# Transposes of q and k straight from the layout of their loads, a new order of the opening, and the second weights asked for ahead of a gate

## The chip, the cores and the metric

The kernel runs on one core of a Trainium2 chip. The metric is the device time of one execution in microseconds (us), the median of several runs; lower is better.

## The reference

Attention with a squared ReLU in place of a softmax, over 8 batches, 12 heads, 448 positions and 64 values a head; its output, laid out as 3584 rows of 768, goes through two weight matrices with a GELU between them. Inputs and output are float32.

```python
scores = scale * np.matmul(q, k.transpose(0, 1, 3, 2))      # scale = 1/sqrt(64)
attn = np.maximum(scores, 0.0) ** 2 / S                     # S = 448
x = np.matmul(attn, v)                                      # (8, 12, 448, 64)
x = x.transpose(0, 2, 1, 3).reshape(B * S, H * D)           # (3584, 768)
h = x @ w_in                                                # (3584, 2048)
out = (0.5 * h * (1.0 + erf(h / sqrt(2)))) @ w_out          # (3584, 768)
```

## The kernel before

**Work and tiles.** All products are in bfloat16. The loads from DRAM are issued by GpSimd (POOL), which converts float32 to bfloat16 on the way. A batch's 12 heads are three groups (g) of four. For each group there are 7 QK steps (L686), each one tile of 896 columns in PSUM; ACT (L698) or DVE (L700) takes the ReLU with the scale, DVE squares it (L707), and after 7 such steps TensorE does AV (L746). Two copies (L400, L402) put its result into `xT`, the transposed input of the first weight product. That product (L800, "F1": 16 atoms of 128 columns of `w_in` a batch, a GELU on ACT behind each) writes a ring `h_sb`. The product with `w_out` (L1203 at first, L1108 from then on) is done on 256 rows at a time, as seven products on sums of blocks in place of eight; the sums of the weights for it (`t_sb`, L1046) are made on DVE once `w_out` is there. For the last three batches the first product is done in that way too (L942, its weight sums at L867).

**Transposes.** QK needs q and k with the head dimension on partitions (`qT`, `kT`, two buffers each). Batches 0 and 1 are transposed on TensorE (L580, L608). From batch 2 on the DMA transposes, issued by SP, do it: three for k, one a group (L632), and four for q, one for each c of 4 (L641), with 128 values to a block. For these a block must hold two heads side by side in an order that the loads of L349 and L434 don't give. So for batch 2 DVE permutes q and k after their load (L529, L540: nine copies) into `pq` and `pk`; for batches 3 to 7 `add_wide` (L459) loads straight into the permuted order, with 6 loads for k and 12 for q a batch, and one for v.

**Order.** A scheduler writes out the order of all instructions when the program is built. The first 263 operations stand by hand in `ORDER` (L69): a letter for the engine (P TensorE, A ACT, D DVE, G POOL, S SP) and the number of the operation. It covers attention of batches 0 and 1, and the first product of batch 0. Every engine works through its own instructions in that order, and an instruction that waits holds up all behind it on its engine. After `ORDER` a planner with costs for each operation (those in `sch.add`), biases and due times picks the order on ACT, DVE and SP. TensorE's order from there on is a fixed list, `pe_q`: eight atoms of the first product of batch 1 (`LEAD`), then for each batch the slots of `slots` (QK, QK, AV, QK, QK; QK, QK, QK), with atoms of the two weight products shared out between them. POOL's list, `pool_q`, is fixed as well: it is the order in which loads are added. Up to eight loads of POOL are under way; the next waits for the landing of the eighth before it.

**Loads.** In POOL's list stand the loads of batch 0, parts of `w_in` between the loads of batch 1, those of batch 2 by group (k, q, v of g 0, 1, 2), the first part of `w_out` (4 of 16 row blocks), then `gate` (L653), a copy of four values of `qT`, with which POOL waits until batch 2 has been transposed, then the two other parts of `w_out` (6 row blocks each), then the loads of batch 3. From then on it goes on by batch: gate of batch b + 1, loads of batch b + 2.

The end of POOL's part of the list for batches 1 and 2 (L1316 to L1335):

```python
for g in range(G):
    add_load(2, g, g + 1)
add_wout(0)
add_steps(steps(1), ATT1_BIAS, True)
...
add_T_dma(2, [[]] * 7)
add_gate(2)
add_wout(1)
add_wout(2)
```

Of the kernel before, what the change touches and what calls it, by code (L numbers as in the profile page):

```python
# [23 lines left out]
FF = 2048  # L24
KD = DM // 128
# [10 lines left out]
T_TWO = 0.72  # L36
# [8 lines left out]
DMA_FREE = 4.54  # L45
# [11 lines left out]
NEAR = 0.5  # L57
# [4 lines left out]
WIDE = 2.0  # L62
# [13 lines left out]
G0 G1 G2 G3 G4 G5 A10 D13 G6 A16 P11 P14 G7 D12 A15 P17 G8 D18 P21 P39 D22 P33 P36 A34 D40  # L76
P19 D20 A37 P23 G9 P42 P48 D24 P54 A43 D35 A49 P51 D44 P25 D38 A52 D41 G117 A55 D53 P45 D50
A26 D47 A46 P57 D56 P69 P66 A58 D70 P27 G118 A67 P29 D59 P63 G119 A28 D71 P60 A64 G120 D68
P78 D61 A62 P75 A79 D65 P81 P31 D30 A76 D80 P96 G121 D32 A97 P72 D77 G122 A82 D98 P129 G123
D74 A73 P90 D130 P84 P108 A91 G124 D83 P131 A85 D109 P93 P141 D132 A94 D92 P102 D95 P105  # L80
P111 A103 D86 P143 D110 G125 A106 D104 P99 A112 D107 G126 A144 P87 D100 A101 D113 A142 P157
P114 D88 G127 A158 D89 P133 D115 A116 G128 P135 D159 A134 P160 P163 D136 P166 A164 P145 D167
A161 D165 P253 A146 D168 D162 P169 P172 G147 A254 P175 A173 D170 P245 G148 A176 D171 P255
A246 D177 G149 D174 P184 P187 A256 P196 A185 G150 D188 P137 P139 A138 P178 D197 G151 A140
D186 P193 P211 G152 D180 P247 A212 G153 D213 P249 A248 D179 A194 D198 G154 P263 A250 D195
D229 G155 P223 P220 A264 D189 P190 S235 A224 D221 P265 G156 A191 D225 P267 A266 D192 D222
P199 P217 A268 P214 D231 A218 P257 S236 D215 A200 D219 P259 A258 D216 D201 P181 P208 A260
P205 D230 A209 P261 D182 P251 D183 A262 D210 A206 D233 P202 A252 S237 D207 D232 P226 D234
A203 D204 S238 S239 P269
# [17 lines left out]
class Scheduler:  # L107
# [151 lines left out]

    def place(self, fixed):  # L260
# [14 lines left out]
        while rest or any(fixed.values()):  # L275
# [7 lines left out]
            for e, v in fixed.items():  # L283
                if v and not (e == "PE" and by.get("PE")):
                    tops.append(self.pick(v[:1]))
# [11 lines left out]
def kernel(  # L297
# [34 lines left out]
    q32 = natpool.tile([KC, 4, HC * D], F32, tag="pq", name="q32")  # L332
    k32 = natpool.tile([128, 2, NK * D], F32, tag="pk", name="k32")

    def get_nat(b):
        if b not in nq:

            tq, tk = ("pq", "pk") if b == 1 else ("nq", "nk")
            nq[b] = natpool.tile([KC, H, NC * D], BF16, tag=tq, name="nq")
            nk[b] = natpool.tile([128, HP, NK * D], BF16, tag=tk, name="nk")  # L340
            vt[b] = vpool.tile([128, HP, NK * D], BF16, tag="v", name="v_sb")

# [4 lines left out]
    def load_q(b, g0, g1, c0=0, c1=NC):  # L347
        get_nat(b)
        nc.gpsimd.dma_start(  # L349
            nq[b][:, 4 * g0 : 4 * g1, c0 * D : c1 * D], q_view(b, g0, g1, c0, c1)  # L350
        )
# [25 lines left out]
    pqk = []  # L377

    def get_p():
        if not pqk:  # L380
            pqk.append(natpool.tile([KC, NC, DM], BF16, tag="pq", name="pq"))
            pqk.append(natpool.tile([128, G, NK * 128], BF16, tag="pk", name="pk"))
        return pqk

# [3 lines left out]
    def get_T(b):  # L388
        if b not in qkT:
            qkT[b] = (  # L390
                tpool.tile([128, HP, S], BF16, tag="qT", name="qT"),
                tpool.tile([128, G, NK * 128], BF16, tag="kT", name="kT"),
            )
        return qkT[b]

# [24 lines left out]
    Pq, Pk, Tq, Tk = {}, {}, {}, {}  # L420
# [3 lines left out]
    def war(b):  # L424

        old = [o for (bb, *_), o in list(Pq.items()) + list(Pk.items()) if bb == b - 1]
        c = {1: -1, 2: 0}.get(b, b - 1)
        old += [o[0] for (bb, *_), o in list(Tq.items()) + list(Tk.items()) if bb == c]
        return old
# [19 lines left out]
    def add_v(b, g0, g1):  # L449
        def fn():  # L450
            get_nat(b)
            nc.gpsimd.dma_start(vt[b][:, 2 * g0 : 2 * g1], kv_view(v, b, g0, g1))  # L452

        old = [o for (bb, *_), o in AV.items() if bb == b - 3]
        o = dma(fn, (g1 - g0) * 4 * S * 256, old)
        for g in range(g0, g1):
            ld_v[b, g] = [o]

    def add_wide(b):  # L459


        def k_fn(e):
            def fn():
                to = get_p()[1].rearrange("p g (i e d) -> e p g i d", e=2, d=D)
                src = kv_view(k, b, 0, G).rearrange("p (g e) (i d) -> e p g i d", e=2, d=D)
                for g in range(G):
                    nc.gpsimd.dma_start(to[e][:, g], src[e][:, g])  # L467

            return fn

        def q_fn(e, j):
            def fn():
                to = get_p()[0].rearrange("p c (g j e d) -> j e g p c d", j=2, e=2, d=D)
                src = q[b].rearrange("(g e j) (p c) d -> j e g p c d", e=2, j=2, c=NC)
                for g in range(G):
                    nc.gpsimd.dma_start(to[j][e][g], src[j][e][g])  # L476

            return fn

        def v_fn():  # L480
            vt[b] = vpool.tile([128, HP, NK * D], BF16, tag="v", name="v_sb")
            nc.gpsimd.dma_start(vt[b], kv_view(v, b, 0, G))

        n = G * 4 * S * 256
        ks = [dma(k_fn(e), WIDE * n / 2, war(b), G) for e in range(2)]
        qs = [dma(q_fn(e, j), WIDE * n / 4, war(b), G) for e in range(2) for j in range(2)]
        old = [o for (bb, *_), o in AV.items() if bb == b - 3]
        o = dma(v_fn, n, old)
        ops = Both(ks), Both(qs)
        for g in range(G):  # L490
            ld_v[b, g] = [o]
            Pk[b, g] = ops[0]
            for c in range(NC):
                Pq[b, g, c] = ops[1]

    class Both:


        def __init__(self, ops):
            self.ops = ops  # L500

        @property
        def done(self):
            ends = [o.done for o in self.ops]
            return None if None in ends else max(ends)

    def add_load(b, g0=0, g1=G):
        if b > 2:
            return add_wide(b)
# [16 lines left out]

    def permute_k(copy, g, src):

        copy(  # L529
            get_p()[1][:, g].rearrange("p (i e d) -> p e i d", e=2, d=D),  # L530
            src.rearrange("p e (i d) -> p e i d", d=D),
        )

    def permute_q(copy, g, c0, c1, src):

        dst = get_p()[0][:, c0:c1, 256 * g : 256 * g + 256].rearrange(
            "p c (j e d) -> e p j c d", j=2, d=D
        )
        for e in range(2):
            copy(dst[e], src[:, 2 * e : 2 * e + 2].rearrange("p j (c d) -> p j c d", d=D))  # L540

    def add_pk(b, g0, g1, after=(), bias=0.0):
        for g in range(g0, g1):
            deps = ld_k[b, g] + list(after)
            deps += [Tk[max(b - 1, 1), x, i][0] for x in range(G) for i in range(NK)]
            Pk[b, g] = sch.add(
                (("DVE", 0.31, 0.43),),
                lambda e, g=g: permute_k(V.tensor_copy, g, nk[b][:, 2 * g : 2 * g + 2]), deps,
                bias=bias,
            )  # L550

    def add_pq(b, g0, g1, c0=0, c1=NC, after=(), bias=0.0):
        for g in range(g0, g1):
            deps = [ld_q[b, g, c] for c in range(c0, c1)] + list(after)
            deps += [Tq[max(b - 1, 1), g, c][0] for c in range(c0, c1)]
            if b == 2:
                deps += [Tq[1, x, c][0] for x in range(G) for c in range(NC)]
            d = 2 * (0.07 + (c1 - c0) * 128 / 3840)

            def fn(e, g=g):  # L560
                permute_q(
                    V.tensor_copy, g, c0, c1, nq[b][:, 4 * g : 4 * g + 4, c0 * D : c1 * D]
                )

            op = sch.add((("DVE", d, d + 0.12),), fn, deps, bias=bias)
            for c in range(c0, c1):
                Pq[b, g, c] = op
# [31 lines left out]
    def add_tq(b, g, c0=0, c1=NC, bias=T_BIAS):  # L599
# [14 lines left out]
        def fn2(e):  # L614
            copy(e, get_T(b)[0][:, 2 * g : 2 * g + 2, c0 * KC : c1 * KC], box[0])
# [11 lines left out]
    def add_T_dma(b, after):  # L627

        after = [list(x) for x in after]
        for g in range(G):  # L630
            def fn(e, g=g):
                nc.sync.dma_start_transpose(  # L632
                    get_T(b)[1][:, g].rearrange("p (i t) -> p i t", t=128), get_p()[1][:, g]
                )

            op = sch.add((("SP", 1.2, 3.0),), fn, [Pk[b, g]] + old_T(b) + after.pop(0), mode="X")
            for i in range(NK):
                Tk[b, g, i] = (op, op)
        for c in range(NC):
            def fn(e, c=c):  # L640
# [813 lines left out]
```

## Time and profile before

| | |
|---|---|
| median of 3 runs | 370.96 us (370.91 to 371.25) |
| the profiled execution | 370.77 us |
| its span, first to last instruction | 368.9 us |
| mean granted TensorE clock | 0.999 |
| busy: TensorE (PE), its weight loads (PEld) | 358.9, 222.1 us |
| busy: DVE, ACT, POOL | 288.3, 200.8, 108.0 us |
| POOL waiting at the gates, in total (5 times) | 64.4 us, the longest 19.2 |
| software DMA queue (POOL's loads) | 74992 packets, 22.47 MB, 58.6% |
| hardware DMA queue (transposes, stores) | 38768 packets, 19.46 MB, 26.8% |

The profile is of one execution. Busy times are those of the engine's own instructions; issuing a DMA takes an engine's queue but isn't counted for SP and ACT. The share of a DMA queue is the time that its packets took, in parts of 16 DMA engines over the stretch. A line such as `PE L686` is an instruction of line 686 on TensorE; `<-` names what the instruction waited for.

### The profile page before, as it was taken

The page shows a single profiled execution, that of the slowest core. Times are in us where ns is not written, and L with a number is a line of the kernel's source. Part 1 is how long each engine was busy: PE and PEld are TensorE (multiplying, and loading weights), DVE is VectorE, ACT ScalarE, POOL GpSimd, SP SyncE. Part 2 cuts the span into 40 slices and gives each one's busy share as a digit, 9 for nine tenths or more (in the row PEclk, how much of TensorE's full clock was granted, in tenths as well). Part 3 has the DMA queues.
Part 4 walks back from the last instruction along what each step waited for, and adds up shares of the span by engine and source line. Part 5 has one row for each costly group of instructions (what it writes and reads, how often), then busy time and mean ns, then how long its engine had stood idle before and what let it go on. Part 6 is the DMA issues. An engine that isn't in the chain of part 4 may idle for free.

```text
span 368.9 us, 8544 instructions
## 1 busy us (share of the span) xinstructions
PE 358.9 (97%) x3557; PEld 222.1 (60%) x3557; DVE 288.3 (78%) x493; ACT 200.8 (54%) x308; POOL 108.0 (29%) x149
## 2 busy tenths in 40 slices
PE   8799999999999999999999999999999999999994
PEld 7566645455544455544455545457886897688663
DVE  2998991789868978987699888888998658665862
ACT  4988865664447845677755588853440353044200
POOL 8666401726087096097095000000000000000000
PEclk9999999999999999999999999999999999999999
DMA  9999999999999999999999960003002301310233
GB/s 174 196 200 204 202 189 134 173 171 131 244 135 167 160 85 172 209 163 154 146 93 133 205 117 2 3 0 87 2 0 88 85 2 29 109 36 2 85 85 88
DMA packets 114166, 42.98 MB, mean 116 GB/s; under 512 B 92816, under 2 KB 110672, under 8 KB 114128
## 3 DMA queue, kind: packets, MB, share of 16 engines
q0 software_dynamic: 74992, 22.47, 58.6%
q1 hardware_dynamic: 38768, 19.46, 26.8%
q8 instruction: 28, 0.46, 0.5%
q10 hardware_dynamic: 368, 0.51, 0.4%
q14 instruction: 10, 0.08, 0.1%
HBM read 45.61 MB, written 11.01 MB: 153 GB/s over the span
## 4 chain that ended last, share of the span: by engine, by line
PE 87%; DMA 4%; DVE 4%; ACT 2%; POOL 1%; issue 1%; DVEq 0%; POOLq 0%; ACTq 0%
PE pso L1108 32%; PE psh L800 24%; PE pb L942 13%; PE ps L686 8%; PE pav L746 6%; PE pso L1203 3%; DMA v_sb<-in_v_dram 2%; DVE a_sq L707 2%; DMA nk<-in_k_dram 2%; ACT a_sq L698 2%; POOL nk L434 0%; POOL v_sb L452 0%; POOL nq L349 0%; PE tp L580 0%; DVE a_sq L700 0%
## 5 line engine op out<-in xcount | busy, mean ns | idle before, releaser
L698 ACT ACTIVATE a_sq<-ps 128x896 bf16<-128x896 f32 (+1 forms) x136 | 117.4, 914 | 44.6 <-PE ps L686 44.5
L707 DVE TENSOR_TENSOR a_sq<-a_sq 128x896 bf16<-128x896 bf16 (+1 forms) x169 | 97.5, 617 | 7.5 <-ACT a_sq L698 7.2
L800 PE MATMUL psh<-xT,win_sb 128*128 128x448 bf16 (+1 forms) x516 | 96.6, 340 | 0.1
L800 PEld LDWEIGHTS <-win_sb 128*128 128x128 bf16 x516 | 47.8, 98 | 45.5 <-issue 10.2
L810 ACT ACTIVATE h_sb<-psh 128x448 bf16<-128x448 f32 x80 | 43.9, 549 | 24.1 <-PE psh L800 23.9
L1108 PEld LDWEIGHTS <-s_sb 128*128 128x128 bf16 x424 | 40.6, 98 | 27.0 <-issue 2.2
L700 DVE TENSOR_SCALAR a_sq<-ps 128x896 bf16<-128x896 f32 x33 | 35.9, 1090 | 18.3 <-PE ps L686 17.8
L686 PE MATMUL ps<-qT,kT 64*64 64x448 bf16 (+1 forms) x756 | 47.3, 336 | 2.2 <-ACT qT L402 0.6
L976 DVE TENSOR_TENSOR part<-pb,part 128x448 f32<-128x448 f32 x60 | 34.6, 619 | 18.4 <-PE pb L942 18.4
L476 POOL DMA_DIRECT2D pq<-in_q_dram x60 | 41.8, 704 | 10.1 <-DVE a_sq L707 6.4
L1108 PEld LDWEIGHTS <-h_sb 128*128 128x128 bf16 x312 | 29.9, 98 | 21.1 <-issue 2.5
L1108 PE MATMUL pso<-wout_sb,s_sb 128*128 128x384 bf16 (+2 forms) x216 | 38.1, 320 | 0.3 <-DVE osb L1142 0.3
L1108 PE MATMUL pso<-wout_sb,h_sb 128*128 128x384 bf16 x208 | 38.1, 326 | 0.0
L1108 PE MATMUL pso<-t_sb,s_sb 128*128 128x384 bf16 x208 | 38.1, 326 | 0.0
L746 PE MATMUL pav<-a_sq,v_sb 64*64 64x448 bf16 (+1 forms) x756 | 36.8, 330 | 0.7 <-ACT a_sq L698 0.4
L686 PEld LDWEIGHTS <-kT 64*64 64x64 bf16 x756 | 18.3, 105 | 24.2 <-issue 17.4
L985 ACT ACTIVATE h_sb<-part 128x448 bf16<-128x448 f32 x36 | 19.8, 578 | 19.9 <-DVE part L976 19.8
L467 POOL DMA_DIRECT2D pk<-in_k_dram x30 | 28.9, 966 | 1.5 <-issue 0.9
L746 PEld LDWEIGHTS <-v_sb 64*64 64x64 bf16 x756 | 21.1, 107 | 13.0 <-issue 2.3
L942 PEld LDWEIGHTS <-win_sb 128*128 128x128 bf16 x288 | 27.6, 98 | 2.2 <-issue 0.4
L1142 DVE TENSOR_TENSOR osb<-pso,p_sb 128x384 f32<-128x384 f32 x39 | 21.7, 556 | 8.2 <-PE pso L1108 5.7
L400 DVE CAST xT<-pav 128x448 bf16<-128x448 f32 (+1 forms) x43 | 23.7, 583 | 4.6 <-PE pav L746 3.9
(62 smaller groups left out, 292.0 us busy)
## 6 DMA issues: line engine op xcount, KB each, us to landing
pk<-in_k_dram POOLq DMA_DIRECT2D x30, 112.0 KB, 4.4
pq<-in_q_dram POOLq DMA_DIRECT2D x60, 56.0 KB, 5.0
v_sb<-in_v_dram POOLq DMA_DIRECT2D x5, 672.0 KB, 9.1
out_dram<-osb SPq DMA_DIRECT2D x8, 336.0 KB, 3.0
wout_sb<-in_moe_w_out_dram POOLq DMA_DIRECT2D x2, 1152.0 KB, 12.1
v_sb<-in_v_dram POOLq DMA_DIRECT2D x9, 224.0 KB, 8.8
out_dram<-osb SPq DMA_DIRECT2D x7, 288.0 KB, 3.4
out_dram<-osb SPq DMA_DIRECT2D x8, 240.0 KB, 3.1
```

The source lines that it names most:

```text
L467: nc.gpsimd.dma_start(to[e][:, g], src[e][:, g])
L476: nc.gpsimd.dma_start(to[j][e][g], src[j][e][g])
L686: nc.tensor.matmul(ps[64 * j : 64 * j + 64, e, x * w : x * w + w], kT[r, g, i * 128 + 64 * j : i * 128 + 64 * j + 64], qT[r, 2 * g + j, co ...
L698: A.activation(ar, ps, AF.Relu, scale=c_att)
L700: V.tensor_scalar(ar, ps, c_att, 0.0, op0=mybir.AluOpType.mult, op1=mybir.AluOpType.max,)
L707: V.tensor_mul(box["a2"][:, :, :used], ar, ar)
L746: nc.tensor.matmul(pav[0][o2 : o2 + 64, e, :w], vt[b][r, 2 * g + e, bass.ts(i, D)], box["a2"][r, e, o : o + w], start=(i == 0), stop=(i == ...
L800: nc.tensor.matmul(ph[:, x * n : x * n + n], win_sb[:, kd, bass.ts(m + x, 128)], xT[b][:, kd, c], start=(kd == 0), stop=(kd == KD - 1),)
L810: A.activation(h_ring()[:, m : m + nm, o + c.start : o + c.stop], box[0][:, :S].rearrange("p (x n) -> p x n", x=nm), AF.Gelu,)
L942: nc.tensor.matmul(bank[name][:, y, z * HS : z * HS + HS], w[:, k, bass.ts(mm, 128)], right()[:, k], start=first and k == 0 and z == 0, st ...
L976: V.tensor_add(get(to), ps(name), get(other))
L1108: nc.tensor.matmul(box[bank][:, n0:n1], left()[:, kf], right[:, kf, n0:n1], start=bool(need) and kf == 0, stop=kf == K2 - 1, skip_group_ch ...
```

## The change

**Layout.** From batch 3 on q and k are loaded as batch 2's were, with one load each (`add_wide`, `Both`, `pq`, `pk`, the permutes and their DVE operations are gone). q gets a tile with one empty column block of 64 ahead of it and one behind; two memsets on POOL clear them. k is transposed with the heads as they lie: a block of 128 holds two neighbouring key blocks of one head (or the last of one head and the first of the next). q is transposed twice, once from the start of the tile and once 64 values further on, so that each q block lands once on the lower and once on the upper 64 partitions; the two results go to the even and odd slots of a `qT` of 49 slots. QK and AV pick their blocks by new indices; their number and sizes are the same.

**Transposes.** A batch has nine on SP in place of seven: for each group k, q from offset 64 ("even", 8 blocks) and q from offset 0 ("odd", 9, 8 and 8 blocks). A group's QK needs the three of its group (`even`, `odd`, and the odd one before). The planner's costs for one are 1.6 and 4.5 us in place of 1.2 and 3.0.

```diff
     def add_T_dma(b, after):
...
+        def turn(dst, src, deps):
+            return sch.add(
+                (("SP", T_STEP, T_TIME),),
+                lambda e: nc.sync.dma_start_transpose(dst(), src()),
+                deps + old_T(b) + after.pop(0), mode="X",
+            )
...
+        def q_src(n, o, k):
+            return lambda: nq[b][:, 128 * n + D * o : 128 * (n + k) + D * o]
...
+        n0, odd = 0, None
         for g in range(G):
...
+            op = turn(k_dst(g), k_src(g), list(ld_k[b, g]))
             for i in range(NK):
                 Tk[b, g, i] = (op, op)
...
+            n = 8 * g + 9
+            even = turn(slots_of(8 * g, 1, 8), q_src(8 * g, 1, 8), lands)
+            prior = odd or even
...
+            odd = turn(slots_of(n0, 0, n - n0), q_src(n0, 0, n - n0), lands + beyond)
+            n0 = n
+            for c, o in enumerate((even, odd, prior, odd)):
+                Tq[b, g, c] = (o, o)
```

**Gate and weights.** The gate copies one value of each of the 49 slots, so it waits for all nine transposes; for batch 2 it now stands behind the second and third part of `w_out`. The slots at which SP may start the transposes of a batch are the same two, five transposes at the first and four at the second (before: four and three).

```diff
     add_wout(0)
     add_steps(steps(1), ATT1_BIAS, True)
-    for g in range(G):
-        add_pk(2, g, g + 1, bias=T_TWO)
-        add_pq(2, g, g + 1, bias=T_TWO)
-    add_T_dma(2, [[]] * 7)
-    add_gate(2)
+    add_T_dma(2, [[]] * 9)
     add_wout(1)
     add_wout(2)
+    add_gate(2)
...
-            add_T_dma(b + 1, [at(b, n + (y >= 4)) for y in range(7)])
+            add_T_dma(b + 1, [at(b, n + (y >= 5)) for y in range(9)])
```

**Order.** `ORDER` is new, 257 operations long. It holds the same work of TensorE and the same loads in the same order of POOL; POOL's list behind it is the one above. Its SP words put five transposes of batch 2 in this order: S233 (q even, g 1), S232 (k, g 1), S230 (q even, g 0), S229 (k, g 0), S231 (q odd, g 0). Its beginning and its last lines:

```diff
+D13 G0 G1 A10 P11 G2 A16 D12 P17 P14 A18 P39 P42 P19 D15 A40 G3 D43 P21 G4 A22 D20 D41 P36 G5
+D44 G6 P54 P33 A37 P25 G7 P48 A34 P23 D55 A49 D24 D26 P51 P57 A52 P63 A58 G8 D56 D35 P69 G9
...
+P220 P214 A180 D207 P217 A244 P245 D183 A221 A215 P253 G153 G154 P211 D210 S230 A218 A246 P223 D186
+D222 A224 G155 D219 P202 A212 D216 A254 A204 D225 P259 P261 A260 P263 A262 A203 D213 S229 P255
+A264 P247 S231 A256 P257 P226 A248 A258 P265 G156
```

**Planner.** Its start of the DMA is 3.05 us in place of 4.54, and `NEAR` is 0.25 in place of 0.5. A new `pick_pe` may take the next atom of a weight product ahead of its turn when the next QK or AV in `pe_q` would wait.

```diff
+    def pick_pe(self, v):
...
+        top = self.pick(v[:1])
+        wait = math.inf if top is None else top[1] - self.free["PE"]
+        if v[0].mode == "F" or wait <= (PULL if self.mode == "F" else PULL_IN):
+            return top
+        nxt = next((o for o in v if o.mode == "F"), None)
+        other = nxt and self.pick([nxt])
+        if other and other[1] - self.free["PE"] <= PULL and other[1] < self.free["PE"] + wait:
+            return other
+        return top
```

**Buffers.** The float32 tiles of the start and the tiles of batch 1 lie in buffers of the weight sums (`t1`, `t2`, `t4`) and of `s1`; the weight sums of the first product take the q tile, the k tile and a `qT` buffer, so that they wait for the last QK of batch 6; v of batch 7 waits for AV of batch 5, and the block sums of batch 6 for the QK of batch 7.

```diff
-        old = [o for (bb, *_), o in AV.items() if bb == b - 3]
+        old = [o for (bb, *_), o in AV.items() if bb == (b - 2 if b == B - 1 else b - 3)]
...
-        last += [o for (bb, *_), o in F1.items() if bb == B - 5]
+        last += [o for (bb, *_), o in QK.items() if bb == B - 2]
...
-        gone = [o for (bb, *_), o in QK.items() if bb == (B - 1 if b == B - 1 else B - 2)]
+        gone = [o for (bb, *_), o in QK.items() if bb == (B - 2 if b == B - 3 else B - 1)]
```

## The prediction, made before the result was known

> **What bounds the kernel now.** I read the page's busy times and chain of waits first, then the stretches of the opening, then the queues at the one place where the change sets new work against old: the hand-over to batch 2, at 43 to 80 us.
>
> ```profile
> PE 358.9 (97%) x3557; PEld 222.1 (60%) x3557; DVE 288.3 (78%) x493; ACT 200.8 (54%) x308; POOL 108.0 (29%) x149
> PE 87%; DMA 4%; DVE 4%; ACT 2%; POOL 1%; issue 1%; DVEq 0%; POOLq 0%; ACTq 0%
> ```
>
> TensorE is busy for 358.9 of 368.9 us and holds 87% of the chain. So little is to be won, and whatever makes TensorE wait is lost in full. Where it isn't busy (stretches; columns are length, then PE, PEld, DVE, ACT, POOL busy, clock, DMA share, GB/s):
>
> ```profile
> 6.00:10.00 4.00, 3.64 (x90) 2.72 (x94) 2.80 (x6) 2.37 (x4) 4.00 (x7) 1.00 1.40 197
> 10.00:20.00 10.00, 7.54 (x204) 5.13 (x204) 9.48 (x19) 9.49 (x16) 7.02 (x11) 1.00 1.47 195
> 20.00:30.00 10.00, 9.43 (x243) 7.35 (x236) 9.37 (x19) 8.81 (x15) 5.91 (x9) 1.00 1.28 203
> 30.00:56.00 26.00, 25.92 (x299) 14.85 (x292) 23.36 (x41) 20.20 (x31) 8.45 (x12) 1.00 1.28 198
> 56.00:100.00 44.00, 43.66 (x363) 22.51 (x361) 30.63 (x47) 24.73 (x39) 16.85 (x22) 1.00 1.40 171
> 100.00:256.00 156.00, 155.50 (x1468) 81.05 (x1467) 133.72 (x222) 100.45 (x142) 60.91 (x80) 1.00 1.07 121
> ```
>
> Idle in the opening: 0.36 + 2.46 + 0.57 + 0.08 = 3.47 us. From 56 to 256 us: 0.34 + 0.50 = 0.84 us. The rest of the idle time is the start and the last stores, which the change leaves alone. In 10 to 20 us DVE (9.48) and ACT (9.49) are full, so the opening is bound by evictions.
>
> Now the hand-over. TensorE, POOL and SP timelines (start, length, engine, line):
>
> ```profile
> 54.70 10.39 PE L800 MATMUL psh<-xT,win_sb 128*128 128x448 bf16 x54
> 65.02 0.57 PE L686 MATMUL ps<-qT,kT 64*64 64x448 bf16 x8
> ```
>
> ```profile
> 43.51 0.76 POOL L372 DMA_DIRECT2D wout_sb<-in_moe_w_out_dram  x1 [0.37 <-DMA nq<-in_q_dram]
> 63.48 0.19 POOL L653 COPY gate<-qT 128x4 bf16<-128x4 bf16 x1 [19.21 <-DMA qT<-pq]
> 63.71 1.65 POOL L372 DMA_DIRECT2D wout_sb<-in_moe_w_out_dram  x2
> ```
>
> ```profile
> 42.96 11.90 SPq L632 DMA_TRANSPOSE kT<-pk  x3
> 54.96 6.94 SPq L641 DMA_TRANSPOSE qT<-pq  x4
> ```
>
> Batch 2's first QK starts at 65.02, and its transposes are all in at 63.48, when the gate fires: a margin of 1.5 us. The two large weight loads start only behind the gate, at 63.71. How transposes (q1) and loads (q0) share the DMA engines is seen in single microseconds (packets, MB, share): first 48 to 49 us, then 53 to 54 us with the first weight part in q0, then transposes alone at 61 to 62 us, then weights alone at 69 to 70 us.
>
> ```profile
> q0 software_dynamic: 205, 0.12, 87.2%
> q1 hardware_dynamic: 204, 0.05, 47.2%
> ```
>
> ```profile
> q0 software_dynamic: 104, 0.16, 94.4%
> q1 hardware_dynamic: 101, 0.03, 24.8%
> ```
>
> ```profile
> q1 hardware_dynamic: 1141, 0.28, 127.7%
> ```
>
> ```profile
> q0 software_dynamic: 135, 0.21, 113.9%
> ```
>
> With both queues filled, they get **one packet each in turn**, whatever a packet holds. A transpose packet is a 256-byte row, a weight packet one row of 768 values. Alone, transposes do up to 1141 packets per us; beside weights, some 101.
>
> **What the Trainium skill says.** "DMA: Bandwidth & Descriptors", Queues, rings and completion order: each DMA engine goes round the queues that have work, one packet at a time. The trace agrees (205 to 204, 104 to 101). Its Rules for kernel authors add that issuing from several engines gives no bandwidth, since all run on the same 16 DMA engines; here weights fall from 135 to 104 per us when transposes run. "TensorE: Matmul & The Clock Gate", Part 1, says that after one idle window of about 3.4 us TensorE runs at half rate until about 3.4 us of work have passed. The trace of before can't show it, for no gap inside it is that long.
>
> **The change, part by part.**
>
> *Loads of batches 3 to 7.* 18 issues a batch (6 of 966 ns, 12 of 701 ns, 14.2 us of POOL) become 2, and two small memsets come. TensorE waits for none of these loads in the list of waits: nothing gained; cover gone, nothing lost. DVE's permutes of batch 2 go (3 x 385 + 6 x 286 ns = 2.9 us at 42 to 54 us, where TensorE is never idle): 0. QK and AV keep count and shape: 0.
>
> *Other buffers.* The weight sums now wait for the last QK of batch 6 (about 217 us; they start at 226.9 anyway); v of batch 7 waits for AV of batch 5 (about 191 us; issued at 198.2 now, nothing behind it on POOL but the end); the batch 6 sums wait for QK of batch 7 (247.9 us; used past 280). All 0.
>
> *Transposes.* A batch has 3 k of 7 blocks x 128 rows = 2688 packets before and after; q goes from 24 blocks x 112 = 2688 to 49 x 112 = 5488, and 7 issues become 9. For batches 3 to 7 the transposes of before end 2.6 to 7 us ahead of their first use (gates at 101.7, 128.9, 157.2, 183.5; first QK at 107.2, 131.5, 161.4, 190.7), but that is set by the slots that SP waits for: k goes at one slot, q some 10 us later at the next. Now five go at the first slot, and a first QK needs three of them; at 950 packets per us (mean of 774 to 1141 at 60 to 63 us) these 2800 packets take 2.9 us plus some 4 of latency, so they are in before the second slot. The other four are for the later groups, over 7 us further on. 8176 packets, 8.6 us in all, with no loads beside them, since POOL's gate holds those back: 0 (if one came late all the same, some 2).
>
> *Batch 2.* The new order puts five transposes on SP: q even of g1, k of g1, q even of g0, k of g0, q odd of g0. The first QK needs the last three, so it needs all five: 4 x 896 + 1008 = 4592 packets. The first can start when q of g1 is in, issued at 37.38 and 9.3 us on its way: 46.7. Packets of the first transpose of before flowed 4 us after issue (42.96 to 47.0), so about 50.3.
>
> *The weights sooner.* POOL issues all three parts of w_out ahead of the gate. Part one went at 43.51, as soon as the eighth DMA before it had landed; the next two follow as theirs land (44.3 and 45.6): about 46.5 instead of 63.7. They pass the gate and batch 3's loads on POOL, and they stand in q0 behind batch 2's loads. In all 16 x 128 = 2048 packets. q0 turned to weights at about 51.5 before; with transposes starting later it does so at about 50.9. At 108 per us (104 and 112 in 53 to 55) the weights last 19.0 us, **to 69.9**. Transposes get as many packets in that time, plus some 90 ahead of it: 2140. The other 2450 then take 2.6 us at 950: 72.5, and 0.6 us to the signal (last packets before 62.9, gate 63.48): **73.1 us**.
>
> TensorE's order behind the opening is fixed: eight atoms of the next product, then this QK, with all else queued behind it. So QK waits until 73.1, where it started at 65.02: **+8.1 us**. The bounds: +5 (part of the weights held back by POOL's limit of eight, or transposes alone at 1141) to +11 (94 packets per us).
>
> *Restart.* The gap is over 9 us, so by the skill's page the clock falls: 3.4 us at half rate is +1.7 us, an estimate; bounds 0 (the clock holds) and 3.4.
>
> *New opening.* Same work for TensorE (16 transposes, 43 QK, 9 AV, 16 products) with 36 mode changes for 35. Going through both orders with durations from the rows (relu one per 0.79 us on ACT, 1.0 on DVE; square 0.53; half copies 0.3), ACT gets its first relu at 7.8 instead of 8.5. The last release that the first product needs (copy of the first k of batch 1, on DVE) comes at 22.0, after 13.7 us of DVE work from 7.45 and 0.8 of waits. So the product starts at about 22.0 instead of 22.73, with 9.32 us of TensorE work done instead of 9.13. Followed to 38 us it is 1.1 to 1.4 ahead: -1.2 us at the first QK of batch 2 (bounds: 0, both engines being full as before; -3.4, all idle time gone). Where QK waits for transposes this **buys nothing**: the wait grows from 8.1 to 9.3.
>
> *Middle.* The six weight sums on DVE (0.95 us each, at 58 to 86 us, one of which waits 2.7 us for w_out) find an idle DVE in the gap, and products pulled ahead can fill short waits for evictions: -0.4 of the 0.84 us (bounds -0.8; +0.5 if pulls add mode changes). The gate of batch 2 fires near 77 instead of 63.5; load 3 then takes about 13 us (to 90) and its first transposes 7 more, against first use at 107.2 + 9: 0.
>
> Sum: 8.1 + 1.7 - 0.4 = +9.4. The profiled execution took 370.8 (span 368.9 and 1.9 around it; the median is 371.0): **380.2 us**.
>
> **The rivals.** *A, the wait above*, 374.5 to 386. *B, the transposes are in time*: only opening and middle count, 370.8 - 1.2 - 0.4 = 369.2, faster. Its place is the same QK, its price nil, and it decides at 63.8 us: 4592 packets between 50.3 and 63.2 are 356 per us. For it: the new transposes need no permute, so they start without DVE (before, the second and third k waited for it). Against it: 101 to 204 per us in every microsecond with loads, and the weights now fill that time. *C, a short wait*: the last part of the weights is held back on POOL. Then 1280 weight packets last to 62.8, the transposes have 1370 done and need 3.4 us more: 66.8, +1.8 without a cold restart, 372.2. Against it: the wait of eight is over by 46. That the weights are not asked for sooner at all is B again, since nothing else holds the transposes up.
>
> **How the numbers follow.** A 0.78, B 0.15, C 0.07. A's upper and lower tenth are cut, C is held: 372 to 384.5; A's own range is 375 to 384.5. A change of 0.2%, 0.74 us, is about what a measurement can tell. A and C are slower, 0.85; B is faster but for a quarter in which the opening gives under half its worth: faster 0.11, same 0.04.
>
> **What would show it.** Right: the first QK of batch 2 waits for a DMA of qT, at about 73 us; q0 and q1 move about 105 packets each per us from 51 to 70; the gate near 77; from then on the pace of before. Wrong: q1 well above q0 in that time, or that QK at 64 without a wait. The opening is judged by the first product (22.0) and the end of the eight atoms (63.8).

## The result, and the profile after

| | before | after |
|---|---|---|
| median | 371.11 us (370.91 to 371.90, 4 runs) | 380.96 us (380.56 to 381.38, 4 runs) |
| ratio, 95% interval | | 1.0261 (1.024 to 1.0283): slower |
| profiled execution, its span | 370.77, 368.9 us | 380.56, 378.4 us |
| mean granted TensorE clock | 0.999 | 0.984 |
| software queue (loads), packets and share | 74992, 58.6% | 30512, 39.7% |
| hardware queue (transposes, stores) | 38768, 26.8% | 55952, 33.2% |

The change takes 9.85 us more; 9.4 more were forecast (380.2 us). First the busy times and the chain of waits on the page of after.

```profile
PE 361.3 (95%) x3557; PEld 222.1 (59%) x3557; DVE 281.1 (74%) x479; ACT 205.0 (54%) x313; POOL 47.7 (13%) x81
...
PE 82%; DMA 8%; SPq 3%; DVE 2%; ACT 1%; POOL 1%; issue 1%; DVEq 0%; POOLq 0%
```

TensorE has as many instructions as before, and its share of the chain fell from 87 to 82%. In its place stand DMA (8% for 4%) and, new, SP's queue (3%): a transfer, and the issuing of it, have come onto the path. POOL's busy time is less than half, which bought nothing, since TensorE had waited for none of it. TensorE's timeline of after shows where (start, length, engine, line; QK is L648 now, the product L761):

```profile
55.20 10.39 PE L761 MATMUL psh<-xT,win_sb 128*128 128x448 bf16 x54
73.01 0.96 PE L648 MATMUL ps<-qT,kT 64*64 64x448 bf16 x8 [7.42 <-DMA qT<-nq]
73.91 2.40 PE L761 MATMUL psh<-xT,win_sb 128*128 128x448 bf16 x6
76.24 0.57 PE L648 MATMUL ps<-qT,kT 64*64 64x448 bf16 x8
```

Before, the same QK began at 65.02 and took 0.57 us, without a wait. Now it waits 7.42 us for a DMA of qT and starts at 73.01, **8.0 us later**. The QK and the six products behind it take 3.23 us (73.01 to 76.24) where they took 1.74 (65.02 to 66.76), **1.5 us more**. From there to the end of the span it is 302.16 us after and 302.14 before: **0.0**. The sum, 9.5 us, is the difference of the two spans.

What the transfer waited for begins on POOL and SP. Here POOL's timeline of after, with the last part of the weights and the gate:

```profile
45.94 0.82 POOL L405 DMA_DIRECT2D wout_sb<-in_moe_w_out_dram  x1 [0.28 <-DMA nk<-in_k_dram]
...
78.30 0.32 POOL L610 COPY gate<-qT 128x49 bf16<-128x49 bf16 x1 [31.54 <-DMA qT<-nq]
```

All the weights are asked for by 46.8, where two of the three parts went behind the gate before (63.71). SP's timeline:

```profile
46.97 1.33 SPq L570 DMA_TRANSPOSE qT<-nq  x1
...
54.24 9.88 SPq L570 DMA_TRANSPOSE qT<-nq  x1
```

The first transpose is issued in 1.33 us, before any packet of that queue moves; the third takes 9.88 us. That SP stands there until the packets ahead have gone is read from these lengths, not shown by a view of its own. What slows those packets is seen in single microseconds of the DMA queues, first 64 to 65 us, where before nothing at all was under way, then 71 to 72 us (packets, MB, share):

```profile
q0 software_dynamic: 112, 0.17, 93.8%
q1 hardware_dynamic: 112, 0.03, 21.7%
```

```profile
q1 hardware_dynamic: 1121, 0.28, 126.8%
```

The first view has one packet each in turn, 112 a microsecond. It is so in every microsecond between 51 and 67: 96 to 121 each, but for 59 to 60 us, where both fall to some 53. The weights run out between 68 and 70 us. By 71 the transposes go **ten times as fast**, 1121 a microsecond, and at 73.01 the QK has what it needs.

The stretches of TensorE in after show the restart (length, PE busy and instructions, clock, DMA share, GB/s):

```profile
70.00:72.00 2.00, 0.00 (x0) 0.50 1.26 233
72.00:74.00 2.00, 0.99 (x9) 0.50 0.99 200
...
76.00:77.00 1.00, 1.00 (x11) 0.92 0.83 149
```

The clock fell at about 69.3, 3.7 us after TensorE had stopped, and came back at about 76.2, after 3.2 us of work. "TensorE: Matmul & The Clock Gate", Part 1, of the Trainium skill gives about 3.4 us for both, and here the trace agrees.

### The profile page after: what moved, and what is told of

The parts are those of the page before. It is cut to its first block, busy times and chain, and to the rows that moved or that the text cites. A ratio compares the mean times of both kernels' runs of the same rounds, so it can differ in the third digit from the quotient of the medians.

```text
span 378.4 us, 8424 instructions
## 1 busy us (share of the span) xinstructions
PE 361.3 (95%) x3557; PEld 222.1 (59%) x3557; DVE 281.1 (74%) x479; ACT 205.0 (54%) x313; POOL 47.7 (13%) x81
## 3 DMA queue, kind: packets, MB, share of 16 engines
q0 software_dynamic: 30512, 22.47, 39.7%
q1 hardware_dynamic: 55952, 23.76, 33.2%
## 4 chain that ended last, share of the span: by engine, by line
PE 82%; DMA 8%; SPq 3%; DVE 2%; ACT 1%; POOL 1%; issue 1%; DVEq 0%; POOLq 0%
PE pso L1075 31%; PE psh L761 19%; PE pb L905 12%; PE ps L648 9%; PE pav L709 7%; DMA nq<-in_q_dram 4%; DMA wout_sb<-in_moe_w_out_dram 3%; SPq L570 3%; PE pso L1170 3%; DMA qT<-nq 1%; ACT a_sq L660 1%; DVE part L939 1%; PE tp L543 1%; POOL nk L461 1%; PE tp L515 0%
## 5 line engine op out<-in xcount | busy, mean ns | idle before, releaser
L660 ACT ACTIVATE a_sq<-ps 128x896 bf16<-128x896 f32 x138 | 119.7, 921 | 40.7 <-PE ps L648 40.3
L669 DVE TENSOR_TENSOR a_sq<-a_sq 128x896 bf16<-128x896 bf16 x169 | 97.9, 617 | 13.1 <-ACT a_sq L660 11.9
L761 PE MATMUL psh<-xT,win_sb 128*128 128x448 bf16 (+1 forms) x516 | 98.0, 343 | 0.0
L761 PEld LDWEIGHTS <-win_sb 128*128 128x128 bf16 x516 | 47.9, 98 | 46.8 <-issue 11.4
L648 PE MATMUL ps<-qT,kT 64*64 64x448 bf16 (+1 forms) x756 | 48.4, 340 | 9.7 <-DMA qT<-nq 7.4
L662 DVE TENSOR_SCALAR a_sq<-ps 128x896 bf16<-128x896 f32 (+1 forms) x31 | 32.9, 1060 | 15.4 <-PE ps L648 15.3
L648 PEld LDWEIGHTS <-kT 64*64 64x64 bf16 x756 | 18.6, 106 | 31.9 <-issue 23.2
L429 DVE CAST xT<-pav 128x448 bf16<-128x448 f32 (+1 forms) x41 | 22.5, 584 | 10.3 <-PE pav L709 9.7
L905 PEld LDWEIGHTS <-ws 128*128 128x128 bf16 x216 | 20.7, 98 | 0.0
L1075 PE MATMUL pso<-t_sb,h_sb 128*128 128x384 bf16 x104 | 19.1, 326 | 0.0
```

The costliest lines, as they stand in the source:

```text
L429: V.tensor_copy(dst, src)
L648: nc.tensor.matmul(ps[64 * j : 64 * j + 64, e, x * w : x * w + w], kT[r, g, i * 128 + 64 * j : i * 128 + 64 * j + 64], moving, start=True, ...
L660: A.activation(ar, ps, AF.Relu, scale=c_att)
L662: V.tensor_scalar(ar, ps, c_att, 0.0, op0=mybir.AluOpType.mult, op1=mybir.AluOpType.max,)
L669: V.tensor_mul(box["a2"][:, :, :used], ar, ar)
L761: nc.tensor.matmul(ph[:, x * n : x * n + n], win_sb[:, kd, bass.ts(m + x, 128)], xT[b][:, kd, c], start=(kd == 0), stop=(kd == KD - 1),)
```

## The experiments

The theory: the weights, asked for ahead of the gate, share the DMA engines packet by packet with the transposes that QK needs. The rivals: the doubled transposes of q alone are too much, wherever the weights stand; the new order of SP or of the opening does it; a halved clock is the larger part. Each kernel's ratio is against the kernel before, whose medians in these runs were 371.01 to 371.02.

**The moved line alone, both ways.** First the change with the gate back ahead of the weights:

```diff
     add_wout(0)
...
     add_T_dma(2, [[]] * 9)
+    add_gate(2)
     add_wout(1)
     add_wout(2)
-    add_gate(2)
```

> The change with one line put back: the gate of batch 2 stands ahead of the second and third part of the second weights again. Weights theory (the weights' packets alternate one to one with the transposes'): only 512 weight packets are left beside the five transposes, so they are in at about 60 us, the first QK of batch 2 starts at about 65.6 without a wait, TensorE's clock doesn't fall there, and what is left is the opening's 0.5 us: 371.5 us (370.9 to 372.3). Theory that the doubled q transposes are the cause: most of the wait stays, over 377 us.

Measured: 373.31 us (372.72 to 375.53), ratio 1.0061 (1.0049 to 1.0073). The wait at QK is gone (it starts at 65.07), and with it 7.65 of the 9.9 us. But it is 1.8 above what was expected. The profiled execution is the slowest of the eight (375.53 us), so the lengths in it are not those of the median. Its TensorE timeline shows a wait that neither kernel had:

```profile
65.07 0.57 PE L648 MATMUL ps<-qT,kT 64*64 64x448 bf16 x8
...
83.62 1.61 PE L1170 MATMUL pso<-wout_sb,h_sb 128*128 128x384 bf16 x6 [3.44 <-DMA wout_sb<-in_moe_w_out_dram]
```

Its POOL timeline says why:

```profile
67.23 0.69 POOL L610 COPY gate<-qT 128x49 bf16<-128x49 bf16 x1 [22.64 <-DMA qT<-nq]
67.88 1.65 POOL L405 DMA_DIRECT2D wout_sb<-in_moe_w_out_dram  x2
```

The gate fires at 67.23, not 63.48: the nine transposes with q doubled are through 3.75 us later than the seven were. They also begin later, at 47.10 instead of 42.96, since the new order on SP puts a transpose of group 1 first. But an earlier beginning buys little: in the kernel with the old opening, further down, the five transposes that the first QK needs are issued from 42.51 and are in at 62.05, against 62.58 and 62.01 in its two siblings, which issue them from 47.79 and 47.16. So it is mainly their number. The weights are asked for 4.2 us later than before, and now it is the first product with `w_out` that waits for them. The added transposes don't hurt the QK; they hurt what stands behind the gate.

Then the kernel before, with nothing but the weights moved ahead of the gate:

```diff
     add_T_dma(2, [[]] * 7)
-    add_gate(2)
     add_wout(1)
     add_wout(2)
+    add_gate(2)
```

> The kernel before with the one line of the change that moves the gate of batch 2 behind all parts of the second weights; its seven transposes, its permutes and its opening stay. Weights theory: the 2048 weight packets last to about 70, some 2850 of 5376 transpose packets are done by then, the rest takes 2.7 us: first QK of batch 2 at about 73.8 in place of 65.0, and 1.5 us for the slow clock after it: 381.4 us (379.5 to 383). Theory of the doubled q transposes: nothing was doubled here, so 371 to 372 us.

Measured: 381.31 us, ratio 1.0285 (1.0268 to 1.0303). Its TensorE timeline (QK is L686 here):

```profile
74.66 0.96 PE L686 MATMUL ps<-qT,kT 64*64 64x448 bf16 x8 [9.45 <-DMA qT<-pq]
```

The old layout, old transposes and old opening, with one line moved, lose **10.3 us**, as much as the whole change (9.85; the intervals overlap). This settles it: the moved line is enough for the whole loss, and the doubling of q isn't needed for it.

**The dose.** Half of the weights behind the gate:

```diff
     add_wout(1)
-    add_wout(2)
     add_gate(2)
+    add_wout(2)
```

> The change with the gate between the second and the third part of the weights, so 1280 weight packets instead of 2048 compete. Weights theory: they end at about 62.2, 1280 transpose packets are done, 3310 left at 950 per us: first QK of batch 2 at about 66.3, 0.7 us late, no slow clock: 372.3 us (371.5 to 374). Theory of the doubled transposes: as the change, 378 to 381 us.

Measured: 374.01 us, ratio 1.0081 (1.0064 to 1.0098). The QK, in the TensorE timeline:

```profile
67.48 0.96 PE L648 MATMUL ps<-qT,kT 64*64 64x448 bf16 x8 [2.44 <-DMA qT<-nq]
```

With 1280 packets of weights in the way instead of 2048, QK starts 5.5 us sooner than in the changed kernel; 67.48 is 1.2 later than expected. The restart was slow here too (0.96, then 2.42 us for six products, clock 0.87 in 60 to 70 us), after no more than 2.44 us of idleness.

Then the weights left as in the change, but the three transposes that the first QK needs put at the head of SP's five:

```diff
-... D192 S233 A242 ... S232 A209 ... S230 A218 ... S229 P255 ... S231 A256 ...
+... D192 S229 A242 ... S230 A209 ... S231 A218 ... S232 P255 ... S233 A256 ...
```

> The change with the five transposes of batch 2 in the order k, q even, q odd of group 0, then k and q even of group 1: the first QK now needs 2800 packets instead of 4592. Weights theory: they still wait for the end of the weights at about 68.5, with 2000 done; 800 left: QK at about 70.2 in place of 73.0: 378.2 us (377 to 379.2). Theory that the order on SP is the cause: no wait, 371.5 us.

Measured: 378.00 us, ratio 1.019 (1.0177 to 1.0203).

```profile
69.17 0.96 PE L648 MATMUL ps<-qT,kT 64*64 64x448 bf16 x8 [4.07 <-DMA qT<-nq]
```

Fewer transposes ahead of the QK, and it comes 3.8 us sooner, with the weights still in the way. Here the first transpose is also issued sooner, at 42.06 instead of 46.97, since it needs loads of group 0 and not of group 1; the two aren't taken apart. So the start of the QK goes with the number of packets on either side, in the direction that one to one sharing has it: 73.01, 69.17, 67.48 and 65.07 us in the changed kernel and these three, within 1.2 us of what was expected each time. SP's order alone can't be the cause: with the gate back in place and that order unchanged, the QK is in time.

**A gate for the five that matter.** A small gate on the five transposes of the first slot, ahead of the weights; the full gate stays behind them:

```diff
-    def add_wout(i):
+    def add_wout(i, deps=()):
...
+        def fn():
+            if deps:
+                nc.gpsimd.tensor_copy(gate[:, :17], get_T(2)[0][:, : 17 * KC : KC])
+            load_wout(kf)
...
-    add_wout(1)
+    add_wout(1, [Tq[2, 0, c][0] for c in range(NC)])
     add_wout(2)
     add_gate(2)
```

> The change with a second, smaller gate: ahead of the second part of the weights POOL copies 17 values of qT, which waits for the five transposes that the first QK of batch 2 needs; the full gate stays where the change has it. Weights theory: the five are in at about 60.5, so no wait at that QK; the weights start at about 60.7 and need 1536 packets at about 114 per us, so they land near 76, ahead of their first use at 78.4; both waits are gone: 370.8 us (370.0 to 371.5). If the first gate's version lost its 2.3 us through anything else than its late weights, 373.

Measured: 378.77 us (377.74 to 380.03), ratio 1.0202 (1.0188 to 1.0215). **A miss by 8 us**, and an instructive one. The two goals were met: QK starts at 65.50 without a wait, and the weights are asked for at 63.03, as before. But the other four transposes of batch 2 now go beside the weights, at their pace, and the full gate fires at 81.67. So the loads of batch 3 are issued from 83.72, and its transposes on SP wait for them. Here SP's timeline, of the slowest of the five executions:

```profile
90.50 8.44 SPq L576 DMA_TRANSPOSE kT<-nk  x3
99.04 4.09 SPq L576 DMA_TRANSPOSE qT<-nq  x3
103.24 0.99 SPq L1042 DMA_DIRECT2D out_dram<-osb  x2
```

Behind them in SP's order stand stores of the output, which nothing holds back but the transposes ahead of them. Until a store is done its buffer isn't free, and the list of waits (total, times, longest) shows how that goes back to TensorE:

```profile
DVE osb L1115 <- DMA out_dram<-osb: 8.9, 1, 8.9
...
PE pso L1081 <- DVE osb L1115: 5.9, 1, 5.9
```

DVE waits for a buffer, TensorE for DVE. A gate is also what spaces the loads on POOL, and SP is a queue like any other: a late transpose delays a store.

The same with the old opening in place of the new (the operations of `ORDER` renumbered, batch 2's transposes at the places of the old ones):

```diff
-D13 G0 G1 A10 P11 G2 A16 D12 P17 P14 A18 P39 P42 P19 D15 A40 G3 D43 P21 G4 A22 D20 D41 P36 G5
+G0 G1 G2 G3 G4 G5 A10 D13 G6 A16 P11 P14 G7 D12 A15 P17 G8 D18 P21 P39 D22 P33 P36 A34 D40 P19
...
```

> As the smaller gate, with the opening of the kernel before (its list of operations renumbered, without the permutes, and the five transposes in the order k, even, odd of group 0, k, even of group 1). Theory that the new opening is worth nothing: as the smaller gate within 0.5 us. Theory of the prediction (the new opening is worth 1.2 us): 1.2 us slower than the smaller gate, about 372.

Measured: 378.92 us, ratio 1.0209 (1.0193 to 1.0225): 0.15 from the one above. But it loses its time in another place. TensorE has no wait for an output buffer here; the DVE and the TensorE timelines show this instead:

```profile
72.79 0.96 DVE L1018 TENSOR_TENSOR t_sb<-wout_sb 128x1536 bf16<-128x1536 bf16 x1 [12.26 <-DMA wout_sb<-in_moe_w_out_dram]
...
74.80 0.76 PE L654 MATMUL ps<-qT,kT 64*64 64x448 bf16 x12 [3.40 <-DVE a_sq L668]
```

In this order a sum of the second weights stands on DVE ahead of the evictions of batch 2's scores. It waits 12.26 us for weights that were asked for at 62.51, and the QK behind it waits for DVE. Since the two kernels lose their time in different places, this pair decides nothing about the opening.

And with one copy on DVE ahead of the operation before it (`D46` ahead of `D65`), in the hope that ACT would wait less:

```diff
-... P60 P78 D65 D46
-A30 A47 ...
+... P60 P78 D46 D65
+A30 A47 ...
```

> As the smaller gate, with one word of the new opening moved: D46, the DVE copy of the first AV result, ahead of D65, one square. The ACT copy of the other half starts only when the DVE copy is done, and TensorE waits up to 0.8 us for it. If that chain is what the prediction missed in the opening: 0.3 to 0.6 us under the smaller gate. If the wait goes to the next eviction: the same within 0.2 us.

Measured: 378.42 us (375.96 to 379.75), ratio 1.0192 (1.0167 to 1.0217). It has the stall of the first of the three, is 0.35 below it, inside their spread, and its first product starts at 25.79, later than in any kernel here, at a clock of 0.55 in 10 to 20 us. It doesn't test what it was made for.

**The restart.** Products of zeros ahead of the waiting QK keep TensorE at work in the gap (their result goes to a tile that QK overwrites). First 80:

```diff
+                if blocks[0] == (2, 0, 0, None):
+                    for _ in range(80):
+                        nc.tensor.matmul(ps[:, 0, :128], zero, zero, start=True, stop=True)
                 for x, (b, g, i, half) in enumerate(blocks):
```

> The change with 80 products of zeros ahead of the first QK of batch 2, into its own PSUM tile before it is written, about 6.7 us of work in the gap. The wait for the transposes stays at about 73. If the slow clock behind the gap costs 1.5 us, it goes: 379.4 us (378.8 to 380.2), and the clock is 1.0 at 73 to 77. If what follows the gap is slow for another reason (evictions, late loads): as the change, 381.

Measured: 381.83 us (379.83 to 383.18), ratio 1.0287 (1.0261 to 1.0313). The 80 took 4.63 us and left 4.36 us of idleness; the clock fell all the same, with 0.96 us for the QK and 2.42 for the six products. Too few, so it said nothing. Then 140:

```diff
-                    for _ in range(80):
+                    for _ in range(140):
```

> As the change with 140 products of zeros in the gap instead of 80: at 0.058 us each they last 8.1 us, to about 73.6, the end of the wait. The clock stays at 1.0 at 66 to 77, and the 1.5 us of slow restart go: 379.5 us (378.8 to 380.5). If they overrun the wait, up to 0.6 more; if the slow stretch isn't the clock's, as the change, 381.

Measured: 380.38 us (380.23 to 380.69), ratio 1.0252 (1.0239 to 1.0266). TensorE's timeline:

```profile
74.46 0.57 PE L651 MATMUL ps<-qT,kT 64*64 64x448 bf16 x8 [0.93 <-DMA qT<-nq]
74.97 1.31 PE L764 MATMUL psh<-xT,win_sb 128*128 128x448 bf16 x6
```

The same QK and six products at their old lengths, the clock 1.00 from 66 to 80: the slow restart *was* the clock, worth 1.5 us. But in this execution QK's transposes came 1.4 us later than in the changed kernel, although the gate fired at the same time (78.19 and 78.30), so the profiled execution gained nothing, and the 0.6 of the median is inside the noise (the intervals of the two ratios overlap). The kernel with 80 shows the same (74.49). In both, the queue of the transposes all but stood still just before: 739 and 709 packets in 72 to 74 us, against 1629 in the changed kernel. Why it did isn't settled.

**The opening alone.** The kernel before with the new opening, its own nine permutes and seven transposes put in at matching places:

```diff
-G0 G1 G2 G3 G4 G5 A10 D13 G6 A16 P11 P14 G7 D12 A15 P17 G8 D18 P21 P39 D22 P33 P36 A34 D40
+D13 G0 G1 A10 P11 G2 A16 D12 P17 P14 A18 P39 P42 P19 D15 A40 G3 D43 P21 G4 A22 D20 D41 P36 G5
...
```

> The kernel before with the new opening alone (its list renumbered; the nine permutes and five transposes of batch 2 put in at about the same amount of TensorE work as before). Prediction's theory: the opening is worth 1.2 us: 369.8 us. Theory from the profiles so far (the first product comes no sooner, since the copies of an AV result wait for one another, and TensorE's clock sometimes falls to half at 13 to 18 us): 371.0 to 371.8 us.

Measured: 372.66 us (372.52 to 373.22), ratio 1.0045 (1.0033 to 1.0057). **It costs 1.6 us** where 1.2 were to be won. The first product, in TensorE's timeline, where it was to come at 22.0 and stood at 22.73 before:

```profile
23.98 1.32 PE L799 MATMUL psh<-xT,win_sb 128*128 128x224 bf16 x12
```

The first QK of batch 2 follows at 65.83 (65.02 before). The profiled execution is the slowest of the five, with a span 2.4 us above that of before, and it loses another 1.6 us behind that QK: 0.5 in short waits between 77 and 260 us (TensorE idle for 1.38 us there, 0.84 before), most of the rest in a longer busy time of TensorE. In 14 to 18 us the clock is at 0.63. To see whether that is the cause, the same with four or eight products of zeros ahead of five QK steps between 9 and 16 us:

```diff
+SPARE = {(0, 1, 4, 0): 4, (0, 1, 0, 0): 4, (0, 1, 6, 0): 8, (0, 2, 1, 0): 4, (0, 0, 2, 1): 4}
...
+                for _ in range(SPARE.get(blocks[0], 0)):
+                    nc.tensor.matmul(ps[:, 0, :128], zero, zero, start=True, stop=True)
```

> As the new opening alone, with 4 to 8 products of zeros ahead of five QK steps at 9 to 16 us, into tiles that are written right after: TensorE is busier where it waits for evictions. If the half clock in 13 to 18 us comes from a TensorE that is too little busy, the clock stays at 1.0 in the opening, and the time is 0.3 to 0.8 us under the new opening alone. If not: the same, or 0.3 more for the added work.

Measured: 373.41 us (372.76 to 374.69), ratio 1.0067 (1.0053 to 1.0082), 0.75 above the one without them. The clock held at 1.00 in all of the opening, and the first product came at 23.80, 0.2 sooner. The 24 added products cost time of their own, but two more readings agree. Of the five executions without them, the two with a granted clock of 1.00 took 372.68 and 372.62 us, among the others (372.52 to 373.22). And in three kernels above with this opening the clock held at 1.00 by itself (the gate first, half of the weights, the three transposes first): their first product came at 23.22, 23.12 and 23.18, still over 1.1 us later than forecast. So the clock is not the larger part of what is missing.

**All the repairs together.** Half of the weights behind the gate, the three needed transposes first, the old opening:

```diff
-D13 G0 G1 A10 P11 G2 A16 D12 P17 P14 A18 P39 P42 P19 D15 A40 G3 D43 P21 G4 A22 D20 D41 P36 G5
+G0 G1 G2 G3 G4 G5 A10 D13 G6 A16 P11 P14 G7 D12 A15 P17 G8 D18 P21 P39 D22 P33 P36 A34 D40 P19
...
     add_wout(1)
-    add_wout(2)
     add_gate(2)
+    add_wout(2)
```

> The change with both cures: the gate between the second and the third part of the weights, and group 0's three transposes first on SP; and with the old opening. Weights theory: 1280 weight packets beside the 2800 that the first QK needs; they end at 62.2, 1520 left, in at about 64.4, so no wait at 65.0; the gate fires near 70, the last part of the weights lands at 78.5 to 80.5 and is needed at 80: 371.0 us (370.3 to 372.5). If the late gate holds batch 3 up as with the smaller gate (stores behind transposes on SP): 374 or more.

Measured: 379.73 us (379.53 to 380.02), ratio 1.0234 (1.0221 to 1.0248): the worse of the two expectations, and more than it said. QK waits only 1.21 us (67.66), but the gate fires at 74.49 and the last weights are asked for at 74.94, 11 us later than before. TensorE then waits 1.5 us for `w_out` and 2.3 us for a copy of `xT` on DVE. That copy stands behind a sum of the weights, which waits 7.76 us for `w_out`, to 84.50: the path of the kernel with the old opening. The clock is at 0.91 and 0.92 in 80 to 90 and 90 to 100 us. What makes up all of its 8.7 us was not taken apart.

None of these kernels beats the one before. The best forms of the change are the first, with the gate ahead of the weights, at 373.3 us, and the one with half of the weights behind it, at 374.0; their intervals overlap.

## Why the prediction was right, point by point

**The wait (+8.1; measured +8.0).** Right in mechanism, place and size. QK was to start at 73.1 and started at 73.01; the queues were to move 105 packets each per us from 51 to 70 and moved 96 to 121 until 67; the weights were to last to 69.9 and ran out from 68 on. The moved line alone in the kernel before (+10.3), and the QK without a wait once it is moved back, isolate it. The gate was to fire near 77 and fired at 78.30. That the start came within 0.1 us of the forecast is luck in part: the weights ended about a microsecond sooner than was worked out, and the transposes still to come took about 4 us from 68 on, where 2.6 stood in the working; the two errors cancel.

**The restart (+1.7; measured +1.5).** Right: the clock was at half until about 76.2, and with TensorE at work in the gap the QK and its products had their old lengths.

**The opening (-1.2, absorbed).** Wrong in sign, and it didn't show in the total because the wait took it up, as the prediction had it. The first product came at 23.67 instead of 22.0, and the eight atoms began at 55.20 (54.70 before), so that QK's wait was 7.4 us, not 9.3. The working put 0.8 us of waits on DVE ahead of the copy of k that releases the first product. DVE's timeline of after has 1.9 us of waits from 7.2 us up to that copy, which ends at 23.6 instead of 22.0; in the kernel with the gate first, whose clock held, it has 1.1 us, and the copy ends at 23.1. The waits of ACT for DVE's copies of an AV result are no reason: up to 56 us they come to 2.5 us in after and in before.

The clock wasn't in the working either. Stretches of TensorE in after:

```profile
14.00:15.00 1.00, 0.63 (x21) 0.86 1.46 193
15.00:16.00 1.00, 1.00 (x27) 0.50 1.44 193
```

It stays at half until 18 us, where before it was 1.00 throughout. In the three kernels with this opening whose clock held, the eight atoms began at 54.65 to 54.76, level with the kernel before (54.70); in a fourth, with the small gate, they began at 55.19. So the half clock is worth some 0.5 us at most, and the 1.2 us that were to be won are missing without it too. What makes up the rest beside DVE's waits was not taken apart. If the wait hadn't been there, this step would have turned the rival of transposes in time (369.2, faster) into a loss.

**The middle (-0.4; measured 0.0).** Half right: the waits were filled, but it bought nothing. From the second QK of batch 2 (66.76 before, 76.24 after) over the next 203 us, TensorE's idle time fell from 0.84 to 0.13 us, and its busy time rose by as much, from 202.4 to 203.1 us, for 1901 and 1902 instructions. Products pulled ahead into waits cut the QK and AV work into more pieces, 74 for 71, so the added changes of mode, the bound named beside this term, may have taken it back; no run shows what one of them costs. In the sum this miss of 0.4 and the small ones of the two terms above nearly cancel, which is luck as well.

**The transposes and loads of batches 3 to 7 (0).** Right in the changed kernel: its list of waits has one wait of TensorE for a transpose, that of batch 2. But the late gate was put at 0 too, and that held only with TensorE 8 us late as well. With QK on time and the gate late, in the kernel with the small gate (the full one fired at 81.67 there), the loss was 7.8 us, nearly as large as with the wait that it replaced.

**What the prediction didn't see** is why the change cannot simply be put right. Its nine transposes are through 3.75 us later than the seven, so weights behind the gate come late (373.3 us), and weights ahead of it slow the transposes tenfold (381 us).

## What to carry to other kernels

Before a load is asked for sooner, list what stands in the other DMA queues at that time and count packets, not bytes: a transfer of many small packets beside one of large packets goes at the pace of the large ones (here 112 a microsecond instead of 1121). When a gate is moved or split, follow everything behind it on POOL, and everything behind the late transfers on the queue that issues them, down to the buffers that a store has to free. Then look at each engine that uses what the gate makes late: on DVE, a sum that waits for its weights holds up the evictions behind it. A wait that is taken away should be costed with the next one, and a gain ahead of a wait that a transfer sets is worth nothing until that wait is gone.

## What the runs showed of the hardware beyond that

TensorE's clock fell to half at 14.7 us in the changed kernel, though TensorE was busy for 2.72 of the 4 us before 14 and 0.63 of the next one, with no gap over 0.61 us. Its share of work alone doesn't decide this: in the three kernels with the same opening whose clock held at 1.00, it was busy for 2.73, 2.69 and 2.66 of those 4 us. The restart was slow after 2.44 us of idleness as well, in the kernel with half of the weights behind the gate. That page of the skill speaks of an idle window of about 3.4 us, and further on of a clock that swings when TensorE pauses often, without a share of work for it. Neither case here has such a window as far as the trace shows, and what decides it stays open.

SP took 1.33 us to issue the first transpose of batch 2 in the changed kernel and 9.88 us for the third, beside the weights; with the gate first, the same third took 3.26 us. In the kernel with all repairs one took 12.18 us. All else that SP is to issue waits that long.
